# Spreading a finite check over six feed-forward steps of an attention and mixture-of-experts kernel

## The chip, the cores and the metric

The kernel runs on one core of a Trainium2 chip. The time is device microseconds of one execution. Runs of the kernel before took 786.82, 789.31 and 791.52 us, so the median is 789.31 us. The engines are named as in the profile: PE is TensorE (its weight loads are listed as PEld), DVE is VectorE, ACT is ScalarE, POOL is GpSimd and SP is SyncE. Each has its own queue of instructions and takes them in order.

## The reference

Three parts follow one another. Attention keeps, in each row of scores, the 32 largest; a soft mixture of experts with 32 slots follows; last comes a feed-forward layer:

```python
kth = np.partition(scores, -top_k, axis=-1)[..., -top_k:-top_k + 1]
scores = np.where(scores >= kth, scores, -1000000000.0)   # softmax, times v
...
c /= c.sum(1, keepdims=True) + 1e-09                      # mixture: (2304 x 32)
x = c @ slot_out                                          # (2304 x 512)
h = x @ w_in                                              # (512 x 2048)
g = np.where(h >= 1, h, np.where(h <= -1, 0.0, (h + 1) ** 2 / 4.0))
out = g @ w_out                                           # (2048 x 512)
```

Sizes: 4 batches of 8 heads, 576 rows, head width 64; 2304 tokens; 8 experts with a hidden width of 1024; feed-forward width 2048. All in 32-bit floats; the two feed-forward weights come in as 64-bit patterns that the kernel narrows itself.

## The kernel before, in words

Attention runs pair of heads by pair of heads, in an order of operations that is written out by hand (ORDER), and takes the first 480 us or so. Experts and mixture follow to about 545 us. The feed-forward stage is the rest, and the change lies in it.

The feed-forward stage doesn't form x. Since x is c times slot_out, it multiplies slot_out by w_in once and gets a small matrix m (held as four tiles m4[0] to m4[3] of 128 partitions by 512 columns, the "converted weight" of the change), and then h is m times c. m4[0] is made ahead of the stage, m4[1] to m4[3] in steps 4, 12 and 20 (m_spread).

Tokens are cut into six blocks of 384 (t from 0 to 5), the feed-forward width into 16 blocks of 128 (f). A step is one pair (t, f); there are 96. The first 32 steps alternate the blocks t = 0 and 1, and behind them each t goes through its 16 f alone, so steps 32 to 47 are t = 2 and steps 48 to 63 are t = 3. The function step(i) issues, in this order:

- for the pair three steps on (GA = 3), emit_h: one matmul into the PSUM tile h_ps (L1096), on ScalarE the half relu and the square (L1098, L1099);
- for the same pair on VectorE, emit_m (L1104, the last reader of h_ps), the rounded copy of the result (L1112) and the difference from it (L1116), tile names rg and ghl;
- for the pair of step i itself, emit_o: nine matmuls (three for each 128 tokens, L1132) that add into o_ps.

At the last f of a block the three o_ps tiles are copied by ScalarE into o_sb (L1144) and stored by SP (L1145); three buffers serve these copies. While i is below 30, the steps also convert the remaining blocks of w_out (prep, tiles tr_l and whl), with work on ScalarE, VectorE and GpSimd.

PSUM tiles of the tag m_ps have two buffers. h_ps, the tiles of m_spread and the transposes of the checks take them in turn.

The kernel checks two things at run time. tell() looks at whether the shortcut that finds the 32 largest held (bad, badm; L990 and L992), ahead of the feed-forward stage. tell_m() looks at whether m is finite: each of the four tiles is multiplied by zero and summed along its columns (L1000), each sum is compared with zero (L1002), the least of the four is taken in each partition (good, L1004), TensorE turns that column into a row (good_ps, L1006), and VectorE takes its least, turns it about, joins it with badm and writes the one integer flag (L1008 to L1011). At the end every engine reads the flag (L1266), and if it is set, a slow version of the whole kernel runs; with these inputs it doesn't.

The order on TensorE, ScalarE, VectorE and GpSimd is that of the program (manual_schedule). SP's order is set by the scheduler from its model of time; weight loads keep their program order.

Of the kernel before, what the change touches and what calls it, by code (L numbers as in the profile page):

```python
# [8 lines left out]
F32 = mybir.dt.float32  # L9
# [5 lines left out]
ALU = mybir.AluOpType  # L15
AX = mybir.AxisListType
# [3 lines left out]
P = 128  # L20
# [28 lines left out]
NC1 = DFF // CW  # L49
# [30 lines left out]
def kernel_body(tc, qT, kT, vP, phi, w1, w2, w_in, w_out, out, fast, flag):  # L80
    nc = tc.nc
# [3 lines left out]
    ident = cpool.tile([P, P], F32, name="ident")  # L85
# [745 lines left out]
    ps = ps_m.tile([P, P], F32, name="si_ps", tag="m_ps")  # L831
# [17 lines left out]
    m4 = [p_m.tile([P, 512], F32R, name=f"m4_{n}") for n in range(4)]  # L849
    wB = [tail.enter_context(tc.tile_pool(name=f"wB{n}", bufs=1)) for n in range(NB)]  # L850
    p_t = tail.enter_context(tc.tile_pool(name="p_t", bufs=1))
# [37 lines left out]
    mx = {}  # L889
# [102 lines left out]
            nc.vector.reduce_max(badm, ps[:1, :], axis=AX.X)  # L992
            mx["badm"] = badm

    def tell_m():
        if fast:
            sums = p_t.tile([P, NC1], F32, name="sums")
            t = p_t.tile([P, 512], F32, name="none", tag="so_sb", bufs=1)
            for n in range(NC1):
                nc.vector.tensor_scalar(t, m4[n].bitcast(F32), 0.0, 0.0, op0=ALU.mult, op1=ALU.add,  # L1000
                                        accum_out=sums[:, n:n + 1])
            nc.vector.tensor_scalar(sums, sums, 0.0, None, op0=ALU.is_equal)  # L1002
            good = p_t.tile([P, 1], F32, name="good")
            nc.vector.tensor_reduce(good, sums, axis=AX.X, op=ALU.min)  # L1004
            ps = ps_m.tile([P, P], F32, name="good_ps", tag="m_ps")
            nc.tensor.transpose(ps[:1, :], good, ident)  # L1006
            goodm = p_t.tile([1, 1], F32, name="goodm")
            nc.vector.tensor_reduce(goodm, ps[:1, :], axis=AX.X, op=ALU.min)  # L1008
            nc.vector.tensor_scalar(goodm, goodm, -1.0, 1.0, op0=ALU.mult, op1=ALU.add)
            nc.vector.tensor_tensor(goodm, goodm, mx["badm"], op=ALU.max)  # L1010
            nc.vector.tensor_copy(flag, goodm)  # L1011
# [15 lines left out]
    def m_rest():  # L1027
        mx["m"] = ps_m.tile([P, 512], F32, name="m_ps1", tag="m_ps")
        for c in range(NHP):
            for n in range(1, NC1):  # L1030
                nc.tensor.matmul(mx["m"][32 * n:32 * n + 32], so128[:, c, 0, :], wtile[(2, 0, 2 * n + c // 2)][c % 2],
                                 start=(c == 0), stop=(c == NHP - 1), tile_position=(0, 32 * n), skip_group_check=True)

    def m_split():
        mhl = slot_view(h1T_slots[0], "mhl", F32R, [P, 2, 512])
        mh, ml = mhl[:, 0], mhl[:, 1]
        both = (slice(32, 64), slice(64, P))
        for rows in both:
            nc.scalar.copy(mh[rows], mx["m"][rows])
        for rows in both:  # L1040
            nc.vector.tensor_tensor(ml[rows], mx["m"][rows], mh[rows].bitcast(F32), op=ALU.subtract)
        return mh, ml

    def m_spread(n, mh, ml):
        rows = slice(32 * n, 32 * n + 32)
        ps = ps_m.tile([P, 512], F32, name="m_ps2", tag="m_ps")
        for k, part in enumerate((mh, ml)):
            sel = twice[rows, 2 - 2 * k:6 - 2 * k].rearrange("p k s -> p (k s)")
            nc.tensor.matmul(ps, sel, part[rows], start=(k == 0), stop=(k == 1), tile_position=(32 * n, 0))
        nc.scalar.copy(m4[n], ps)  # L1050
# [19 lines left out]
    def prep(f, k):  # L1070
        x64 = wtile[(4, 0, f)]
        hf = x64[:, :, 1].bitcast(F32)
        if k == 0:
            preps[f] = slot_tiles(tr_slots[f % 3], "tr_l", I32)[0]
        t, r = preps[f][:, 0], preps[f][:, 1]
        tf = t.bitcast(F32)
        if k == 0:
            nc.scalar.activation(tf, hf, AF.Abs)
            nc.scalar.activation(r.bitcast(F32), x64[:, :, 0].bitcast(U32), AF.Identity, bias=two, scale=2.0 ** -51)
        elif k == 1:  # L1080
            nc.vector.tensor_scalar(tf, tf, 2.0 ** -15, None, op0=ALU.max)
            nc.vector.tensor_scalar(t, t, 3, None, op0=ALU.logical_shift_left)
            nc.gpsimd.tensor_tensor(t, t, r, op=ALU.add)  # L1083
        elif k == 2:
            nc.vector.scalar_tensor_tensor(t, x64[:, :, 1], SIGN, t, op0=ALU.bitwise_and, op1=ALU.bitwise_or)
            wo_t[f] = slot_tiles(w_slots[f], "whl", F32R)[1]
        elif k == 3:
            nc.scalar.copy(wo_t[f][0], tf)
        else:
            nc.vector.tensor_tensor(wo_t[f][1], tf, wo_t[f][0].bitcast(F32), op=ALU.subtract)  # L1090
            del preps[f]

    def emit_h(s_):
        t, f = s_
        ph = ps_m.tile([P, 512], F32, name="h_ps", tag="m_ps")[:, :BLK]
        nc.tensor.matmul(ph, m4[f // 4][:, f % 4 * P:(f % 4 + 1) * P], cT[t // 3][:, t % 3 * BLK:(t % 3 + 1) * BLK], start=True, stop=True)  # L1096
        r, g = (x[:, :BLK] for x in ring_tile("g", g_slots, "rg", F32))
        nc.scalar.activation(r, ph, AF.Relu, bias=half, scale=0.5)  # L1098
        nc.scalar.activation(r, r, AF.Square)  # L1099
        gs[s_] = ph, r, g  # L1100

    def emit_m(s_):
        ph, r, g = gs[s_]
        nc.vector.scalar_tensor_tensor(g, ph, 1.0, r, op0=ALU.max, op1=ALU.min)  # L1104
        gs[s_] = g, [x[:, :BLK] for x in ring_tile("g", g_slots, "ghl", F32R)]

    def emit_c(s_, on):
        g, (gh, gl) = gs[s_]
        if on is nc.scalar:
            nc.scalar.copy(gh, g)  # L1110
        else:
            nc.vector.tensor_copy(gh, g)  # L1112

    def emit_d(s_):
        g, (gh, gl) = gs[s_]
        nc.vector.tensor_tensor(gl, g, gh.bitcast(F32), op=ALU.subtract)  # L1116
        gs[s_] = gh, gl
# [6 lines left out]
    def emit_o(t, f, rows):  # L1124
        if f == 0:
            pos[t] = [ps_f.tile([P, DM], F32, name=f"o_ps{t}_{n}", tag=("o_ps", "e_ps")[t % 2]) for n in range(NS)]
        gh, gl = gs[t, f]
        wh, wl = wo_t[f]
        for n in rows:
            sl = slice(n * P, (n + 1) * P)  # L1130
            for k, (a, w) in enumerate(((gh, wh), (gh, wl), (gl, wh))):
                nc.tensor.matmul(pos[t][n], a[:, sl], w, start=(f == 0 and k == 0),  # L1132
                                 stop=(f == NF - 1 and k == 2))
            if f == NF - 1:
                o = ring_tile("o", o_slots, "o_sb", F32)[0]
                dst = out[t * BLK + n * P:t * BLK + (n + 1) * P, :]
                if (t, n) == (NT // BLK - 1, NS - 1):
                    a, z = slice(0, DM // 2), slice(DM // 2, DM)
                    nc.scalar.copy(o[:, a], pos[t][n][:, a])
                    nc.vector.tensor_copy(o[:, z], pos[t][n][:, z])  # L1140
                    nc.scalar.dma_start(dst[:, a], o[:, a])
                    nc.sync.dma_start(dst[:, z], o[:, z])
                else:
                    nc.scalar.copy(o, pos[t][n])  # L1144
                    nc.sync.dma_start(dst, o)  # L1145
# [7 lines left out]
    def step(i):  # L1153
        t, f = steps[i]
        nxt = steps[i + GA] if i + GA < len(steps) else None

        def work(*ks):
            for k in ks:
                for x in todo.get((i, k), ()):
                    prep(x, k)  # L1160

        if i == 2:
            m_rest()
            mhl.extend(m_split())
        if i == 40:
            tell_m()
        if i % 8 == 4 and i // 8 < NC1 - 1:
            m_spread(i // 8 + 1, *mhl)
        if i in (0, 2):
            emit_o(t, f, range(NS))  # L1170
        if nxt:
            emit_h(nxt)
        work(4, 2, 1)
        late_g = behind.pop() if behind else None
        if late_g:
            emit_c(late_g, nc.scalar)
        work(3, 0)
        if nxt:
            emit_m(nxt)
        if late_g:  # L1180
            emit_d(late_g)
        if nxt:
            if any((j, 0) in todo for j in (i, i - 1)):
                behind.append(nxt)
            else:
                emit_c(nxt, nc.vector)
                emit_d(nxt)
        if i not in (0, 2):
            emit_o(t, f, range(NS))
# [60 lines left out]
    for i in range(len(steps) - NLAST):  # L1250
        step(i)
# [72 lines left out]
```

## Time and profile before

| | |
|---|---|
| median of three runs | 789.31 us |
| profiled execution, its time | 789.28 us |
| profiled execution, span from first to last instruction | 787.5 us |
| mean granted TensorE clock (share of full speed) | 0.978 |
| TensorE matmul busy | 748.9 us, 95% of the span |
| TensorE weight loads busy | 548.6 us, 70% |
| VectorE busy | 638.4 us, 81% |
| ScalarE busy | 619.7 us, 79% |
| GpSimd busy | 467.2 us, 59% |

The busy shares are averages over stages with different limits. In the page's chain of work that ended last, the o_ps matmuls of L1132 are the largest entry, with 23% of the span; from 548 us on the chain is nearly all theirs. The clock is given as a share of 2.4 GHz: 1.00 is the upper of its two levels, and about 0.50 the lower, 1.2 GHz; a stretch with both lies between.

### The profile page before, as it was taken

The page shows a single profiled execution, that of the slowest core. Times are in us where ns is not written, and L with a number is a line of the kernel's source. Part 1 is how long each engine was busy: PE and PEld are TensorE (multiplying, and loading weights), DVE is VectorE, ACT ScalarE, POOL GpSimd, SP SyncE. Part 2 cuts the span into 40 slices and gives each one's busy share as a digit, 9 for nine tenths or more (in the row PEclk, how much of TensorE's full clock was granted, in tenths as well). Part 3 has the DMA queues.
Part 4 walks back from the last instruction along what each step waited for, and adds up shares of the span by engine and source line. Part 5 has one row for each costly group of instructions (what it writes and reads, how often), then busy time and mean ns, then how long its engine had stood idle before and what let it go on. Part 6 is the DMA issues. An engine that isn't in the chain of part 4 may idle for free.

```text
span 787.5 us, 15936 instructions
## 1 busy us (share of the span) xinstructions
PE 748.9 (95%) x5023; PEld 548.6 (70%) x5023; DVE 638.4 (81%) x2918; ACT 619.7 (79%) x1312; POOL 467.2 (59%) x516
## 2 busy tenths in 40 slices
PE   4899999999999999999999998897999998999996
PEld 2477677777777777777777777333677876888885
DVE  5999999999999999999999973163588866666663
ACT  4799999999999999999999985162699953555552
POOL 2899999999999999999999990020122100000000
PEclk8899999999999999999999999899999998999999
DMA  7414304303312320220220346999500010101101
GB/s 225 146 52 147 130 18 147 135 24 142 134 60 102 134 93 20 80 94 15 96 82 15 90 145 189 347 403 408 215 0 2 29 52 2 41 0 41 37 4 44
DMA packets 31725, 81.50 MB, mean 103 GB/s; under 512 B 5648, under 2 KB 6544, under 8 KB 31632
## 3 DMA queue, kind: packets, MB, share of 16 engines
q1 hardware_dynamic: 31344, 79.94, 28.7%
q8 instruction: 41, 0.67, 0.4%
q14 instruction: 52, 0.43, 0.2%
q10 hardware_dynamic: 288, 0.46, 0.2%
HBM read 71.25 MB, written 8.91 MB: 102 GB/s over the span
## 4 chain that ended last, share of the span: by engine, by line
PE 58%; DVE 19%; ACT 7%; POOL 6%; DMA 5%; issue 2%; SPq 1%; ACTq 0%; DVEq 0%; POOLq 0%
PE o_ps L1132 23%; PE av_ps L502 8%; PE s_ps L294 5%; PE pt_ps L461 5%; DVE cand L318 5%; DMA w<-in_moe_w_dram 4%; DVE top L424 4%; PE x_ps L294 3%; POOL ssb L450 3%; DVE cand L323 2%; PE h_ps L1096 2%; DVE top L325 2%; POOL mb L377 2%; DVE mb L374 2%; PE av_ps L500 1%
## 5 line engine op out<-in xcount | busy, mean ns | idle before, releaser
L1132 PE MATMUL o_ps<-whl,ghl 128*128 128x512 f32 x864 | 219.3, 399 | 0.0
L1132 PEld LDWEIGHTS o_ps<-whl,ghl 128*128 128x128 f32 x864 | 163.4, 191 | 36.0 <-issue 0.8
L450 POOL TENSOR_TENSOR ssb<-ssb,pen 128x576 f32<-128x576 f32 x141 | 180.2, 1283 | 2.5
L318 DVE MAX8 cand<-ssb 128x8 f32<-128x82 f32 (+1 forms) x1008 | 163.7, 235 | 5.7 <-ACT ssb L309 5.7
L502 PE MATMUL av_ps<-v_sb,ptb 128*128 128x65 f32 (+1 forms) x1280 | 143.4, 262 | 0.0
L502 PEld LDWEIGHTS av_ps<-v_sb,ptb 128*128 128x128 f32 (+1 forms) x1280 | 137.7, 182 | 5.8 <-issue 5.8
L1098 ACT ACTIVATE rg<-h_ps,half 128x384 f32<-128x384 f32 x96 | 55.6, 579 | 78.2 <-PE h_ps L1096 78.1
L377 POOL TENSOR_SCALAR mb<-ssb,top 128x576 bf16<-128x576 f32 x64 | 110.2, 1721 | 0.9 <-DVE top L325 0.9
L294 PE MATMUL s_ps<-kt,qt 64*128 64x288 f32 x512 | 100.0, 468 | 8.8 <-ACT ssb L309 4.4
L309 ACT COPY ssb<-s_ps 128x576 f32<-128x576 f32 x144 | 95.7, 665 | 11.3 <-PE s_ps L294 9.9
L461 PE MATMUL pt_ps<-ident,ssb 128*128 128x128 f32 x640 | 100.3, 279 | 2.5 <-ACT ptb L477 2.4
L1083 POOL TENSOR_TENSOR tr_l<-tr_l 128x512 int32<-128x512 int32 x16 | 21.1, 1318 | 127.5 <-PE so L968 42.4
L1104 DVE SCALAR_TENSOR_TENSOR rg<-h_ps,rg 128x384 f32<-128x384 f32 x96 | 53.3, 555 | 53.1 <-ACT rg L1099 53.1
L461 PEld LDWEIGHTS pt_ps<-ident,ssb 128*128 128x128 f32 x640 | 72.0, 146 | 30.3 <-ACT rs L485 6.8
L477 ACT COPY ptb<-pt_ps 128x512 f32<-128x512 f32 x128 | 77.9, 608 | 3.8 <-PE pt_ps L461 3.7
L453 ACT ACTIVATE ssb<-ssb,kn 128x576 f32<-128x576 f32 x96 | 78.4, 816 | 0.7 <-POOL ssb L450 0.6
L447 ACT ACTIVATE pen<-ssb,kn 128x576 bf16<-128x576 f32 x96 | 75.3, 809 | 1.7 <-POOL kn L443 0.9
L424 DVE MAX8 top<-x_ps 128x8 f32<-128x584 f32 x96 | 72.7, 757 | 2.2 <-PE x_ps L408 1.9
L325 DVE MAX8 top<-cand 128x8 f32<-128x56 f32 x432 | 72.8, 205 | 0.1
L294 PEld LDWEIGHTS s_ps<-kt,qt 64*128 64x128 f32 x512 | 39.9, 190 | 34.5 <-ACT ssb L309 10.9
L414 POOL TENSOR_TENSOR w<-ssb,mb 128x576 f32<-128x576 f32 x48 | 61.5, 1281 | 0.4 <-DVE mb L374 0.4
L1116 DVE TENSOR_TENSOR ghl<-rg,ghl 128x384 fp32r<-128x384 f32 x96 | 55.3, 576 | 6.0
(231 smaller groups left out, 1282.5 us busy)
## 6 DMA issues: line engine op xcount, KB each, us to landing
w<-in_moe_w_dram SPq DMA_DIRECT2D x52, 512.0 KB, 6.8
x<-in_moe_w_in_dram SPq DMA_DIRECT2D x16, 512.0 KB, 3.8
w<-in_moe_w_out_dram SPq DMA_DIRECT2D x16, 512.0 KB, 10.2
w<-in_moe_w_dram SPq DMA_DIRECT2D x24, 256.0 KB, 5.4
kt<-in_k_dram SPq DMA_DIRECT2D x15, 360.0 KB, 4.3
v_sb<-in_v_dram SPq DMA_DIRECT2D x16, 325.0 KB, 6.9
qt<-in_q_dram SPq DMA_DIRECT2D x15, 320.0 KB, 5.0
out_dram<-o_sb SPq DMA_DIRECT2D x17, 256.0 KB, 2.2
```

The source lines that it names most:

```text
L294: nc.tensor.matmul(o, q[us], k[us, c:c + o.shape[-1]], start=True, stop=True, tile_position=(j * D, 0), skip_group_check=True)
L309: nc.scalar.copy(ssb[:, 0] if u[1] == NR else ssb[:, :, hf], st.pop((u, hf))[:, :, :HS])
L318: nc.vector.max(st[u]["cand"][:, j, 8 * g:8 * g + 8], row(u, j)[:, S * g // NSEG:S * (g + 1) // NSEG])
L325: nc.vector.max(t8, cand)
L377: nc.gpsimd.tensor_scalar(kept(u, j), row(u, j), t_u, None, op0=ALU.is_ge)
L424: nc.vector.max(st[u]["top"][:, j, TOPU:], src)
L450: nc.gpsimd.tensor_tensor(row(u, j), row(u, j), st.pop((u, "pen", j)), op=ALU.subtract)
L453: nc.scalar.activation(row(u, j), row(u, j), AF.Exp, bias=st[u]["kn"][:, j, 0:1], scale=0.125)
L461: nc.tensor.transpose(pt[:, c, :], pr[:, c0:c0 + P], ident)
L477: nc.scalar.copy(st[u, "ptb", j], st.pop((u, "pt", j)))
L502: nc.tensor.matmul(o, pj[:, c, sl], v_sb[:, 4 * jj + c, :], start=False, stop=(c == NR - 1), skip_group_check=True)
L1132: nc.tensor.matmul(pos[t][n], a[:, sl], w, start=(f == 0 and k == 0), stop=(f == NF - 1 and k == 2))
```

## The change

tell_m is given a number k and does one piece for each: k from 0 to 3 sums one tile of m4, k = 4 compares the sums and takes the least, k = 5 does the transpose and all that follows it. The tiles that pass from piece to piece (sums, good) are kept in the dictionary mx. step(i) calls it at i = 40, 44, 48, 52, 56 and 60, each time ahead of the rest of the step, where the kernel before called the whole at i = 40. The last sum is at step 52, the comparison at 56, the transpose at 60.

```diff
-    def tell_m():
-        if fast:
-            sums = p_t.tile([P, NC1], F32, name="sums")
+    def tell_m(k):
+        if not fast:
+            return
+        if k < NC1:
+            if k == 0:
+                mx["sums"] = p_t.tile([P, NC1], F32, name="sums")
             t = p_t.tile([P, 512], F32, name="none", tag="so_sb", bufs=1)
-            for n in range(NC1):
-                nc.vector.tensor_scalar(t, m4[n].bitcast(F32), 0.0, 0.0, op0=ALU.mult, op1=ALU.add,
-                                        accum_out=sums[:, n:n + 1])
-            nc.vector.tensor_scalar(sums, sums, 0.0, None, op0=ALU.is_equal)
-            good = p_t.tile([P, 1], F32, name="good")
-            nc.vector.tensor_reduce(good, sums, axis=AX.X, op=ALU.min)
+            nc.vector.tensor_scalar(t, m4[k].bitcast(F32), 0.0, 0.0, op0=ALU.mult, op1=ALU.add,
+                                    accum_out=mx["sums"][:, k:k + 1])
+        elif k == NC1:
+            nc.vector.tensor_scalar(mx["sums"], mx["sums"], 0.0, None, op0=ALU.is_equal)
+            good = mx["good"] = p_t.tile([P, 1], F32, name="good")
+            nc.vector.tensor_reduce(good, mx["sums"], axis=AX.X, op=ALU.min)
+        elif k == NC1 + 1:
             ps = ps_m.tile([P, P], F32, name="good_ps", tag="m_ps")
-            nc.tensor.transpose(ps[:1, :], good, ident)
+            nc.tensor.transpose(ps[:1, :], mx["good"], ident)
             goodm = p_t.tile([1, 1], F32, name="goodm")
             nc.vector.tensor_reduce(goodm, ps[:1, :], axis=AX.X, op=ALU.min)
...
-        if i == 40:
-            tell_m()
+        if i % 4 == 0 and i >= 40:
+            tell_m(i // 4 - 10)
```

## Rows read from the trace of the kernel before

**Rows 1.** Chain of waits, 640 to 662 us: start, duration (us), engine, tile, line, count.

```profile
644.23 2.10 PE o_ps L1132 x9
...
649.40 0.61 DVE none L1000 x2
...
652.43 0.17 DVE good L1004
...
652.64 0.37 PE good_ps L1006
...
653.34 3.84 PE o_ps L1132 x9
```

**Rows 2.** Busy time by stretch: stretch, length, engines' busy time (count), clock, DMA.

```profile
644.23:646.50 2.27, 2.27 (x12) 1.86 (x11) 1.48 (x4) 1.11 (x2) 0.00 (x0) 1.00 0.00 0
646.50:653.34 6.84, 2.80 (x13) 2.05 (x12) 5.32 (x15) 1.11 (x2) 0.00 (x0) 0.80 0.00 0
653.34:657.50 4.16, 4.16 (x11) 3.28 (x11) 1.91 (x6) 1.10 (x2) 0.00 (x0) 0.51 0.01 2
657.50:659.77 2.27, 2.27 (x11) 1.87 (x11) 0.92 (x2) 1.10 (x2) 0.00 (x0) 1.00 0.04 11
...
662.06:707.39 45.33, 45.33 (x201) 37.28 (x201) 29.53 (x61) 23.57 (x43) 0.00 (x0) 1.00 0.05 18
```

**Rows 3.** Timeline around step 40: start, duration, engine, line, instruction, idle before it.

```profile
646.17 0.34 PE L1096 MATMUL h_ps<-cT,m 128*128 128x384 f32 x1
...
646.35 2.26 PE L1132 MATMUL o_ps<-whl,ghl 128*128 128x512 f32 x9
...
647.72 0.56 DVE L1104 SCALAR_TENSOR_TENSOR rg<-h_ps,rg 128x384 f32<-128x384 f32 x1 [0.66 <-ACT rg L1099]
...
648.84 0.56 DVE L1116 TENSOR_TENSOR ghl<-rg,ghl 128x384 fp32r<-128x384 f32 x1
649.32 0.68 DVE L1000 TENSOR_SCALAR_CACHE_REDUCE none<-m 128x512 f32<-128x512 f32 x1
...
650.04 0.69 DVE L1000 TENSOR_SCALAR_CACHE_REDUCE none<-m 128x512 f32<-128x512 f32 x1
...
652.23 0.17 DVE L1002 TENSOR_SCALAR sums<-sums 128x4 f32<-128x4 f32 x1
...
652.64 0.37 PE L1006 MATMUL good_ps<-ident,good 128*1 128x128 f32 x1 [4.04 <-DVE good L1004]
...
653.05 0.28 DVE L1008 TENSOR_REDUCE goodm<-good_ps 1x1 f32<-1x128 f32 x1 [0.47 <-PE good_ps L1006]
...
653.72 0.14 DVE L1011 CAST flag<-goodm 1x1 int32<-1x1 f32 x1
```

**Rows 4.** Timeline of TensorE around the transpose of the other check.

```profile
514.92 0.27 PE L990 MATMUL bad_ps<-ident,bad 128*1 128x128 f32 x1
515.12 3.64 PE L968 MATMUL so<-w,h1T 128*32 128x512 f32 x32
```

**Rows 5.** Busy time by stretch: an earlier idle, the steps behind it, forty steady microseconds.

```profile
548.43:552.39 3.96, 3.96 (x12) 3.19 (x12) 3.26 (x7) 1.10 (x2) 0.00 (x0) 0.60 1.03 409
545.65:548.07 2.42, 0.00 (x1) 0.03 (x1) 1.23 (x3) 1.06 (x3) 0.00 (x0) 1.00 1.03 413
...
560.00:600.00 40.00, 38.94 (x169) 30.78 (x168) 32.19 (x64) 37.50 (x73) 9.06 (x7) 1.00 0.04 17
```

**Rows 6.** Timeline of TensorE behind an m_spread: h_ps and its wait.

```profile
564.73 0.44 PE L1096 MATMUL h_ps<-cT,m 128*128 128x384 f32 x1 [0.57 <-DVE rg L1104]
```

**Rows 7.** Instruction groups by line, VectorE, 608 to 646 and 646.5 to 657.5 us.

```profile
L1082 DVE TENSOR_SCALAR tr_l<-tr_l 128x512 int32<-128x512 int32 x3 | 1.3, 427 | 0.1
...
L1000 DVE TENSOR_SCALAR_CACHE_REDUCE none<-m 128x512 f32<-128x512 f32 x4 | 2.7, 684 | 0.1
```

**Rows 8.** Waits of SP's queue (total, times, longest) and the page's output stores.

```profile
SPq L1266 <- DVE flag L1011: 21.8, 1, 21.8
...
out_dram<-o_sb SPq DMA_DIRECT2D x17, 256.0 KB, 2.2
```

## The prediction, made before the changed kernel ran

> **What bounds the kernel now.** I read the chain of waits first, since it says which engine ends last. From 644 us on it is one pattern [rows 1]: a feed-forward step is nine o_ps matmuls of L1132 (2.10 us in the chain) behind one h_ps matmul, and TensorE goes from one group to the next. Once, at step 40, the chain leaves TensorE: it runs through VectorE's ghl L1116, the sums of L1000 and the minimum of L1004, and comes back by the transpose good_ps of L1006. The next group takes 3.84 us in place of 2.10.
>
> Second, the busy time by stretch [rows 2]. Twenty undisturbed steps last 45.33 us, so a step is 45.33 / 20 = 2.267 us; TensorE is busy in all of it at a granted clock of 1.00, while VectorE has 1.48 us of work in a step of 2.27. The two disturbed stretches last 6.84 and 4.16 us. In the second the granted clock is 0.51, the lower of the two levels (1.2 GHz), and directly behind it 1.00 again.
>
> Third, the timeline of step 40, which says who waits for what [rows 3]. TensorE sat idle for 4.04 us ahead of good_ps. Its last work before was the group that starts at 646.35 and takes 2.26, so it came to the transpose at 648.6. VectorE began the first sum only at 649.32, because the three operations of step 39's rg and ghl stand ahead in its queue, and its chain up to good ended at 652.6. So the step waits for VectorE's place in line (0.7 us) and for the chain of six small results (3.3 us). Everything of TensorE's program behind the transpose waits with it. VectorE and ScalarE have nothing to do that would end later.
>
> **What the disturbance costs now.** The stretch from 646.50 to 657.50 holds two steps: 6.84 + 4.16 - 2 x 2.267 = 6.47 us above two normal ones [rows 2]. Of that 4.04 is idle [rows 3]; the rest, 2.43, is the transpose itself and work at the lower clock: 4.16 - 2.27 = 1.89 in the second step, 0.5 around the transpose and the h_ps behind it.
>
> **Part by part.** No instruction is added or removed. The four sums, the comparison with the minimum, and the transpose with its four small operations move from step 40 to the starts of steps 40, 44, 48, 52, 56 and 60. No DMA is issued by them; the flag that two queues read comes later (below).
>
> The sums, steps 40 to 52. Each enters VectorE's queue ahead of that step's rg L1104. It costs 650.04 - 649.32 = 0.72 us from start to start [rows 3]. VectorE waits 0.66 us for ScalarE before each L1104 [rows 3], and this idle time is the cover. Without the check the next L1104 would have started 2.267 after 647.72, at 649.99; behind one sum VectorE is free at 650.04, so L1104 is 0.05 late. The buffers ahead decide whether TensorE sees it. A step makes the operands of the step three later: they were ready at 648.84 + 0.56 = 649.40, and their matmuls would start at 646.35 + 3 x 2.267 = 653.15 in an undisturbed run, 3.75 us later. The two h_ps buffers leave a margin as well: L1104 ends at 647.72 + 0.56 = 648.28, and that buffer is next needed by the h_ps two steps on, 646.17 + 4.53 = 650.70, 2.4 us later. Cost 0. The bounds: below, nothing, since the sums leave VectorE's total work as it is; above, 4 x 0.72 = 2.9 us, if each sum went straight to TensorE. I take 0, because the margin is five times a sum, and three normal steps without a sum follow each, in which the lag is worked off.
>
> At this place stands a row that another price would contradict: tensor_scalar over 128x512 took 427 ns for L1082 and 684 for the summing L1000 [rows 7]. The Trainium skill (VectorE: DVE Perf Modes, The perf-mode tier table) lets tensor_scalar on fp32 in SBUF run at twice the base rate; L1082 looks like that, L1000 does not. By the rule a sum would fit into the idle time with no lag, and the third rival below would have no price; by the row it just fails to fit. I go by the row.
>
> Comparison and minimum, step 56: from 652.23 to the end of L1004, some 0.37 us of VectorE, inside the 0.66 us of idle. Cost 0; if the cover went, 0.37.
>
> The transpose, step 60. It waits for good, which VectorE finished four steps, 9 us, earlier; so TensorE does not stop. Behind it in the queue stand h_ps and nine o_ps matmuls of the step. Its price in a running stream is that of bad_ps, the same instruction for another check: 514.92 to 515.12, 0.20 us [rows 4]. It also takes one turn of the two-buffer PSUM ring. The h_ps behind it now needs the buffer of the step before, not of two steps before. L1104 frees that 2.11 us after its h_ps (646.17 to 648.28), and the next h_ps comes 2.267 + 0.20 = 2.47 after it: margin 0.36 us, no wait. In the earlier steps where such an extra PSUM tile went in while VectorE was also converting weights, the h_ps behind it waited 0.57 us [rows 6]. So the transpose costs 0.20 at least and 0.20 + 0.57 = 0.77 at most; I take 0.20, since VectorE has no conversion left by then. The four small operations (653.05 to 653.86, 0.81 us) stand ahead of one L1104 on VectorE. The transpose ends before VectorE is through with the step before, so they do not wait, and they make that L1104 0.15 late, inside the 3.75.
>
> The flag. SP waited 21.8 us for it, between the sixth and the seventh output store, and read it at 653.9 [rows 8]. Step 40 would begin at 646.17 + 2.267 = 648.44, so the flag comes at about 648.44 + 20 x 2.267 + 1.8 = 695.6. If SP's read keeps its place, the three stores of the third token block wait until then; they land some 2.2 us after their issue [rows 8], by about 699.5. Their buffers are wanted again when the first rows of step 63 are done, about 648.44 + 23 x 2.267 + 0.20 + 1.0 = 701.8. Cost 0, with 2 us to spare. TensorE, VectorE and ScalarE read the flag only after their last work.
>
> **Sum.** -6.47 + 0 + 0 + 0.20 = -6.27 us. The profiled execution took 789.28 us (span 787.5), which is the median of the runs, 789.31, to 0.03. So 789.28 - 6.27 = **783.0 us**, 0.8% faster.
>
> **Rivals.**
> Only the idle goes. If the lower clock after the stall had another cause, 1.89 us would remain: 784.9. For it: the clock record lies beside the stall and does not prove cause. Against: the other long idle of this stage, 2.42 us, was also followed by a slow stretch, at 0.60, while forty steady microseconds ran at 1.00 [rows 5]. Chance 0.05.
>
> The pieces hold TensorE where they now stand. Each costs what it takes on VectorE: 4 x 0.72 + 0.37, and 0.57 more at the transpose, 3.8 us in all: 786.8. For it: at those steps VectorE has 1.48 + 0.72 = 2.20 of 2.27 us to do. Against: the margins of 3.75 and 2.4 us. Chance 0.07.
>
> Slower. The four sums make TensorE pause through the PSUM ring, and every pause lowers the clock for a step: 0.72 + 1.89 = 2.6 us four times, 10.4, so 793.4. It decides from three such pauses on (7.8 against 6.27). The place is the h_ps of each sum step. Against: h_ps waits of 0.57 us in the weight-conversion steps [rows 6] lie in forty microseconds that show 1.00 throughout [rows 5]; a pause would have to be several times longer. The Trainium skill (TensorE: Matmul & The Clock Gate, A second HAM failure mode: psum-queue depth-cycling) describes just this, short idles from cycling PSUM buffers that make the clock swing; by that rule the earlier ring waits should show it, and the trace does not agree. Chance 0.03.
>
> The change gives nothing that shows, because the time is taken elsewhere: SP's later flag read holds stores and through them the copies that empty PSUM. It needs the landing 2 us later than worked out, and then has the 3.75 us margin before it. Time 789, chance 0.02.
>
> **How the numbers follow.** Forecast 0.83; rivals 0.05, 0.07, 0.03, 0.02. A measurement of this kernel tells a change from none at about 0.5%, 3.9 us; the runs of before span 786.8 to 791.5. The forecast's 6.3 us lies outside that, but with this scatter I give it 0.06 of its 0.83 to be read as within 0.5%. Faster: 0.77 + half of the first rival = 0.80. Slower 0.03. Same 0.17. Range: 783.0 less 2.4 for the scatter is 780.6; above, the first rival (784.9) with 1.7 of the scatter gives 786.6 and takes in the transpose's upper bound (783.6).
>
> **What would show it.** In the trace of the changed kernel: no TensorE idle above some tenths between 640 us and the last group; granted clock 1.00 throughout; step 40 to step 59 each 2.27 us; step 60 2.47. L1104 late by 0.05 to 0.2 us at steps 40, 44, 48, 52 and 60 and on time one step later. The flag read at about 695. I am wrong if h_ps waits for L1104 behind the transpose, if the clock falls again, or if the end of the span moves by less than 4 us with the stall gone.

## The result, and the profile after

The changed kernel took 782.39 us (median of six runs, 781.57 to 783.26); the kernel before, 788.82 beside it (786.82 to 791.52). The ratio is 0.9916, 95% interval 0.9896 to 0.9937: 6.4 us less, against 6.3 forecast. The profiled execution took 783.15 us, with a span of 781.3.

The chain of waits of the kernel after, around step 60 (start, duration, engine, tile, line, count), answers to [rows 1]:

```profile
691.56 2.09 PE o_ps L1136 x9
693.65 0.11 PE good_ps L1010
693.76 0.18 PE h_ps L1100
693.94 2.10 PE o_ps L1136 x9
```

From 584 us to the last o_ps group the chain no longer leaves TensorE, and the transpose is 0.11 us of it. The busy time by stretch (stretch, length, busy time of the engines, clock, DMA) answers to [rows 2]; the rows are twenty steps from step 40 on, without the transpose; from the o_ps group of step 59 to that of step 60, with the transpose; the step behind it; and the rest up to the last groups:

```profile
648.52:693.82 45.30, 45.30 (x202) 37.19 (x202) 32.12 (x70) 23.57 (x43) 0.00 (x0) 1.00 0.05 18
691.40:693.77 2.37, 2.37 (x12) 1.86 (x12) 1.50 (x4) 1.11 (x2) 0.00 (x0) 1.00 0.00 0
693.77:696.04 2.27, 2.27 (x11) 1.86 (x11) 2.03 (x8) 1.10 (x2) 0.00 (x0) 1.00 0.00 0
696.20:766.39 70.19, 70.19 (x312) 57.82 (x311) 45.71 (x93) 37.19 (x68) 0.00 (x0) 1.00 0.06 23
```

The twenty steps that now hold the sums take 45.30 us, as twenty undisturbed ones did (45.33), at clock 1.00. From the start of one o_ps group to the next, step 60 takes 2.37 in place of 2.27. The timeline of steps 40 and 60 answers to [rows 3]:

```profile
648.59 0.56 DVE L1120 TENSOR_TENSOR ghl<-rg,ghl 128x384 fp32r<-128x384 f32 x1
649.07 0.68 DVE L1002 TENSOR_SCALAR_CACHE_REDUCE none<-m 128x512 f32<-128x512 f32 x1
...
649.73 0.56 DVE L1108 SCALAR_TENSOR_TENSOR rg<-h_ps,rg 128x384 f32<-128x384 f32 x1
...
651.98 0.56 DVE L1108 SCALAR_TENSOR_TENSOR rg<-h_ps,rg 128x384 f32<-128x384 f32 x1 [0.64 <-ACT rg L1103]
...
693.49 0.27 PE L1010 MATMUL good_ps<-ident,good 128*1 128x128 f32 x1
693.49 0.19 PEld L1100 LDWEIGHTS h_ps<-cT,m 128*128 128x128 f32 x1 [0.15 <-DVE rg L1108]
...
694.37 0.27 DVE L1012 TENSOR_REDUCE goodm<-good_ps 1x1 f32<-1x128 f32 x1
...
695.14 0.56 DVE L1108 SCALAR_TENSOR_TENSOR rg<-h_ps,rg 128x384 f32<-128x384 f32 x1
```

The sum at 649.07 fills VectorE's idle time: the L1108 behind it shows no wait, and the next has its 0.64 us of idle again. At step 60 no TensorE matmul waits. The weight load of h_ps shows 0.15 us of idle, which the profile puts down to L1108. That L1108 had ended some 0.16 us before (it started at 692.77 and took 0.56), and the load started together with the transpose at 693.49; so the row doesn't show a wait for the PSUM ring. In SP's waits (total, times, longest) the flag comes later, as in [rows 8]:

```profile
SPq L1270 <- DVE flag L1015: 27.8, 1, 27.8
```

It was read at 695.2, so SP waited from 667.4 on.

### The profile page after: what moved, and what is told of

Read it like the earlier page. It is cut to its first block, busy times and chain, and to the rows that moved or that the text cites. A ratio compares the mean times of both kernels' runs of the same rounds, so it can differ in the third digit from the quotient of the medians.

```text
span 781.3 us, 15935 instructions
## 1 busy us (share of the span) xinstructions
PE 746.4 (96%) x5023; PEld 547.2 (70%) x5023; DVE 638.0 (82%) x2918; ACT 619.8 (79%) x1312; POOL 467.2 (60%) x516
## 4 chain that ended last, share of the span: by engine, by line
PE 64%; DVE 17%; ACT 7%; POOL 7%; DMA 3%; issue 2%; ACTq 0%; POOLq 0%; DVEq 0%; SPq 0%
PE o_ps L1136 25%; PE av_ps L502 9%; PE s_ps L294 6%; PE pt_ps L461 5%; DVE cand L318 5%; DVE top L424 4%; PE x_ps L294 3%; POOL ssb L450 3%; PE h_ps L1100 2%; PE h L945 2%; POOL mb L377 2%; DVE cand L323 2%; DVE top L325 2%; DVE mb L374 2%; PE av_ps L500 1%
## 5 line engine op out<-in xcount | busy, mean ns | idle before, releaser
L1108 DVE SCALAR_TENSOR_TENSOR rg<-h_ps,rg 128x384 f32<-128x384 f32 x96 | 53.4, 556 | 47.9 <-ACT rg L1103 47.8
```

## The experiments

Medians are set against runs of the kernel before on the same chip and in the same rounds; 1 us is 0.13%. Executions of one kernel scatter by some 2 us, so each kernel is also read by one stretch of its trace: from the start of the second o_ps group of the feed-forward stage to the start of the last 27 o_ps matmuls, as the chain of waits gives it. It leaves out what varies earlier, with one exception: in the double sums the second o_ps group itself still ran partly at the lower clock (2.82 us in place of 2.25), so that stretch holds some 0.6 us from there. The kernel before took 788.82 us beside the kernel after, 789.23 beside the first four experiments and 789.33 beside the next four.

| kernel | median us | ratio to before, 95% | stretch us |
|---|---|---|---|
| before | 789.23 | | 773.07 - 552.39 = 220.68 |
| after | 782.39 | 0.9896 to 0.9937 | 766.39 - 552.13 = 214.26 |
| no check | 782.49 | 0.9909 to 0.9948 | 764.43 - 550.25 = 214.18 |
| sums together at step 40 | 782.62 | 0.9909 to 0.9936 | 765.64 - 551.06 = 214.58 |
| transpose at once, step 56 | 783.75 | 0.9922 to 0.9952 | 767.08 - 551.46 = 215.62 |
| before, wait filled | 787.13 | 0.9969 to 0.9992 | 769.67 - 551.10 = 218.57 |
| nine transposes | 785.24 (one run) | | 768.72 - 553.64 = 215.08 |
| longer wait, step 56 | 787.03 | 0.9956 to 0.9987 | 769.15 - 550.55 = 218.60 |
| double sums at step 40 | 787.53 | 0.9969 to 1.0000 | 770.57 - 551.29 = 219.28 |

**No check.** In the kernel after, the pieces are taken out:

```diff
-        if i % 4 == 0 and i >= 40:
-            tell_m(i // 4 - 10)
+        if i == 60 and fast:
+            nc.vector.tensor_copy(flag, mx["badm"])
```

> The kernel after with the whole finite check of m left out: the flag is written from badm alone, at step 60. Theory (the spread pieces cost TensorE nothing but one transpose of 0.1 to 0.2 us): 782.2 to 782.3 us, not to be told from the kernel after (782.4); step 60 takes 2.27 us in place of 2.38. Rival (each piece holds TensorE for what it takes on VectorE, 3.8 us in all): 778.6.

Measured 782.49 us; the stretch is 214.26 - 214.18 = 0.08 us shorter, and the theory expected 0.1 to 0.2. So the check costs TensorE some 0.1 us where it now stands, and another place for it could win no more than that. The rival's 778.6 falls.

**Sums together, transpose late.** The spread is undone and only the transpose's new place kept:

```diff
-        if i % 4 == 0 and i >= 40:
-            tell_m(i // 4 - 10)
+        if i == 40:
+            for k in range(NC1 + 1):
+                tell_m(k)
+        if i == 60:
+            tell_m(NC1 + 1)
```

> The kernel after with the four sums, the comparison and the minimum together at step 40, and only the transpose left at step 60. Theory (the wait of TensorE was for the transpose; the margins ahead carry a late VectorE): the chain of 3.3 us makes L1108 of step 40 2.6 us late; the h_ps two steps on needs its buffer 2.4 us after it was normally free, so TensorE waits 0.2 to 0.5 us at step 42 and the clock stays 1.00: 782.6 to 782.9. Rival (the spreading is what brought the gain, and a chain of 3.3 us on VectorE stalls TensorE wherever the transpose stands): near 788.8, with a stretch at the lower clock.

Measured 782.62 us; the stretch is 0.32 us longer than after. The timeline of steps 40 to 42, and the busy time from the o_ps group of step 41 to that of step 42:

```profile
651.15 0.16 DVE L1007 TENSOR_REDUCE good<-sums 128x1 f32<-128x4 f32 x1
651.23 0.55 DVE L1108 SCALAR_TENSOR_TENSOR rg<-h_ps,rg 128x384 f32<-128x384 f32 x1
651.83 0.19 PEld L1100 LDWEIGHTS h_ps<-cT,m 128*128 128x128 f32 x1 [0.45 <-DVE rg L1108]
```

```profile
649.57:652.11 2.54, 2.53 (x12) 1.78 (x11) 2.33 (x8) 1.11 (x2) 0.00 (x0) 1.00 0.00 0
```

The h_ps two steps on did wait for its buffer, and cost 2.54 - 2.27 = 0.27 us at clock 1.00. So moving the transpose alone brings 220.68 - 214.58 = 6.10 us of the 6.42, and with it moved, spreading the sums adds the other 0.32.

**Transpose at once.** Everything as after, but the transpose follows the minimum in step 56:

```diff
-        if i % 4 == 0 and i >= 40:
+        if i % 4 == 0 and 40 <= i < 60:
             tell_m(i // 4 - 10)
+        if i == 56:
+            tell_m(NC1 + 1)
```

> The kernel after with the transpose at step 56, directly behind the comparison and the minimum of the same step. Theory (TensorE waits at the transpose until VectorE has come through its queue): VectorE is free 0.9 us into the step and needs 0.37, so TensorE sits idle about 1.3 us. If the clock stays at 1.00 the time is 783.7; if it falls as it did behind an idle of 2.4 us, 785.6 to 786.1. The theory says the idle; which of the two the clock does is open, since waits of 0.57 us left it at 1.00. Rival (the sums alone were the cost and the place of the transpose is free): 782.4, no idle.

Measured 783.75 us, as the theory said for a clock that stays; the stretch is 1.36 us longer than after. The timeline's transpose, and the stretch behind it:

```profile
685.07 0.27 PE L1010 MATMUL good_ps<-ident,good 128*1 128x128 f32 x1 [1.13 <-DVE good L1007]
```

```profile
685.35:687.62 2.27, 2.27 (x11) 1.87 (x11) 1.57 (x6) 1.11 (x2) 0.00 (x0) 1.00 0.00 0
```

The chain is 0.37 us, yet TensorE idles 1.13: the rest is VectorE's own work of the step before, ahead in its queue. In this execution an idle of 1.13 us left the clock at 1.00.

This kernel is also the other half of the change by itself: the sums are spread, and the transpose still follows at once. It brings 220.68 - 215.62 = 5.06 us. So either half alone wins most of the 6.42, and the gains overlap: moving the transpose is worth 6.10 us with the sums together and 1.36 with the sums spread; spreading the sums is worth 5.06 or 0.32.

**The wait, filled.** In the kernel before, matmuls without a use run in the wait:

```diff
-            ps = ps_m.tile([P, P], F32, name="good_ps", tag="m_ps")
-            nc.tensor.transpose(ps[:1, :], good, ident)
+            ps = ps_m.tile([P, 512], F32, name="good_ps", tag="m_ps")
+            for _ in range(16):
+                nc.tensor.matmul(ps, m4[0][:, :P], m4[0], start=True, stop=True)
+            nc.tensor.transpose(ps[:1, :P], good, ident)
             goodm = p_t.tile([1, 1], F32, name="goodm")
-            nc.vector.tensor_reduce(goodm, ps[:1, :], axis=AX.X, op=ALU.min)
+            nc.vector.tensor_reduce(goodm, ps[:1, :P], axis=AX.X, op=ALU.min)
```

> The kernel before with 16 extra matmuls of 128x512 (into the PSUM tile that the transpose then overwrites) ahead of the transpose at step 40, so that TensorE works through the wait; at 0.23 us each they fill 3.7 of the 4.04 us. Nothing is left out. Theory (the lower clock came from the idle): no stretch below 1.00 behind step 40; the wait itself stays; 788.8 less 2.3 to 2.4 is 786.4 to 786.5. Rival (the lower clock has another cause than the idle, so only the idle counts): the slow step of 4.16 us stays, 788.8.

Measured 787.13 us, ratio 0.998: less than before, by 0.6 to 2.4 us. The stretch is 220.68 - 218.57 = 2.11 us shorter. The transpose's row, and the stretches with the wait and behind it:

```profile
651.41 0.27 PE L1008 MATMUL good_ps<-ident,good 128*1 128x128 f32 x1 [0.38 <-DVE good L1004]
```

```profile
645.11:651.69 6.58, 6.20 (x28) 4.78 (x28) 5.10 (x15) 1.11 (x2) 0.00 (x0) 1.00 0.00 0
651.69:653.97 2.28, 2.28 (x12) 1.87 (x11) 1.58 (x6) 1.11 (x2) 0.00 (x0) 1.00 0.03 7
```

With TensorE at work the transpose still starts 651.41 - 645.11 = 6.30 us behind the start of the group before it (6.29 in the kernel before [rows 3]), but the step behind it takes 2.28 us at clock 1.00, where it took 4.16 at 0.51 [rows 2]. The lower clock came from the idle.

**Nine transposes.** In the kernel after:

```diff
-            nc.tensor.transpose(ps[:1, :], mx["good"], ident)
+            for _ in range(9):
+                nc.tensor.transpose(ps[:1, :], mx["good"], ident)
```

> The kernel after with the transpose of step 60 issued nine times, into the same tile. One was forecast at 0.20 us from another check's row; the chain of the kernel after shows 0.11. If a transpose costs 0.11 in this stream, step 60 grows by 0.9 us to 3.3; if 0.20, by 1.6 to 4.0; if the one was partly hidden or a wait for the PSUM ring was in it, by less than 0.5.

One run took 785.24 us (its feed-forward stage began later; its stretch is 0.82 us longer than after). The timeline of TensorE:

```profile
694.94 1.15 PE L1011 MATMUL good_ps<-ident,good 128*1 128x128 f32 x9
...
695.84 0.42 PE L1101 MATMUL h_ps<-cT,m 128*128 128x384 f32 x1
```

Eight more cost 0.82 / 8 = 0.10 us each, so 0.10 to 0.11 is the price in this stream and 0.20 was too much.

**A longer wait.** The kernel with the transpose at step 56, with two sums more ahead of the comparison:

```diff
         elif k == NC1:
+            for n in range(2):
+                t = p_t.tile([P, 512], F32, name="none", tag="so_sb", bufs=1)
+                nc.vector.tensor_scalar(t, m4[n].bitcast(F32), 0.0, 0.0, op0=ALU.mult, op1=ALU.add,
+                                        accum_out=mx["sums"][:, n:n + 1])
```

> The kernel with the transpose at step 56 directly behind comparison and minimum, and two further sums (of tiles 0 and 1 again) ahead of these, so that TensorE's idle ahead of the transpose grows from 1.13 by 2 x 0.72 to 2.6 us. Theory (idle and the fall of the clock behind it are separate prices, and an idle of 1.1 us is too short for the fall while 2.4 us mostly, not always, brings it): 785.2 us where the clock stays, 786.6 to 787.1 where it falls; the median nearer the upper. Rival (only idles as long as 4 us lower it, the start of the stage has another cause): 785.2.

Measured 787.03 us (785.09 to 790.40), at the upper value. The transpose's row, and the two stretches behind it:

```profile
685.61 0.27 PE L1014 MATMUL good_ps<-ident,good 128*1 128x128 f32 x1 [2.59 <-DVE good L1011]
```

```profile
685.90:689.30 3.40, 3.40 (x11) 2.72 (x11) 2.18 (x7) 1.11 (x2) 0.00 (x0) 0.63 0.01 2
689.30:691.97 2.67, 2.67 (x11) 2.17 (x11) 1.05 (x3) 1.10 (x2) 0.00 (x0) 0.83 0.01 3
```

An idle of 2.59 us was followed by steps of 3.40 and 2.67 us: 1.5 us above normal. The rival, that only idles near 4 us lower the clock, falls.

**Double sums.** The kernel with the sums together, each sum done twice (the tile of sums is made once):

```diff
-            if k == 0:
+            if "sums" not in mx:
                 mx["sums"] = p_t.tile([P, NC1], F32, name="sums")
...
-            for k in range(NC1 + 1):
+            for k in (0, 1, 2, 3, 0, 1, 2, 3, NC1):
                 tell_m(k)
```

> The kernel with all sums at step 40 done twice, eight in all, then comparison and minimum; the transpose stays at step 60. VectorE's chain is 8 x 0.72 + 0.37 = 6.1 us, and L1108 of step 40 is 5.5 us late. Theory (the h_ps ring is what ends last, with a margin of 2.2 to 2.4 us): TensorE waits 3.1 to 3.3 us at the h_ps of step 42, and by its length the clock falls behind it: 787 to 788 (785.6 if the clock stayed). Rival (the operands made three steps ahead end last, margin 3.75): a wait of 1.75 us at the o_ps of step 43, 784.2 to 785.6.

Measured 787.53 us. The row of the h_ps that waited, and the stretch behind it:

```profile
655.49 0.69 PE L1100 MATMUL h_ps<-cT,m 128*128 128x384 f32 x1 [2.92 <-DVE rg L1108]
```

```profile
655.98:659.31 3.33, 3.33 (x11) 2.68 (x11) 2.98 (x7) 1.10 (x2) 0.00 (x0) 0.65 0.02 5
```

TensorE waits for a buffer of the h_ps ring, 2.92 us, not 1.75 for operands. The ring, with its margin of 2.4 us, is what a late VectorE meets first.

**Another idle, filled.** A version that could beat both: in the kernel after, TensorE idles 2.4 us ahead of the third h_ps of the feed-forward stage. Matmuls without a use fill it; they write the o_ps tiles of t = 0, which are therefore made earlier.

```diff
-        if f == 0:
+        if f == 0 and t not in pos:
...
+    pos[0] = [ps_f.tile([P, DM], F32, name=f"o_ps0_{n}", tag="o_ps") for n in range(NS)]
+    for k in range(10):
+        nc.tensor.matmul(pos[0][k % NS], m4[0][:, :P], cT[0][:, :DM], start=True, stop=True)
     emit_h(steps[2])
```

> The kernel after with ten extra matmuls of 128x512 ahead of the third h_ps of the feed-forward stage, where TensorE sits idle for 2.4 us in every trace (they write o_ps tiles that the first real group then overwrites). Nothing is left out. At 0.23 us each they fill 2.3 us. In the kernel after the step behind this idle ran at a low clock: 4.10 us from its first o_ps group to the second, against 2.80 in the run without the check, where the clock stayed at 1.00 behind the same idle. Theory (the low clock follows from TensorE's idle, in most runs but not all): clock 1.00 there, 1.3 us less in most runs: 781.0 to 781.4 in the median, and less scatter between runs. Rival (idle and low clock only coincide): no change, 782.4.

Measured 781.81 us (781.55 to 784.51), ratio 0.9895 to 0.9927: not told apart from after. So both were run in the same rounds:

> The kernel after, unchanged, on the same chip and in the same rounds as the next kernel, so that the two can be compared directly. Theory: 782.4 us; runs with the clock down behind the idle of 2.4 us at the start of the stage lie 1.3 us above the others.

> The kernel with the ten extra matmuls in the idle at the start of the feed-forward stage, again. Theory: the clock stays at 1.00 there, and the median is 1.0 to 1.3 us below that of the kernel after in the same rounds. Rival (the median of the kernel after already has most runs with the clock up, or the fill costs what it saves): within 0.5 us of it.

Measured 783.38 us (782.06 to 784.80) for the kernel after and 783.34 (782.34 to 784.73) with the fill. No gain; the theory's 1.0 to 1.3 us didn't come, and the rival's "within 0.5 us" holds. In this second profile of the kernel after the clock stayed up behind the same idle (stretch 214.30 us), so there was nothing to win in that execution. In the ten profiles of this document without the fill, the idle there was 2.42 or 2.43 us each time; the stretch behind it took 3.67 to 4.11 us at a clock of 0.58 to 0.70 in seven, and 2.79 or 2.80 us at 1.00 in three. In both profiles with the fill it took 2.79 or 2.80 at 1.00. So the fill may well save a part of a microsecond on average; six runs of each, which scatter by 2.4 to 2.7 us, don't show it and don't exclude it.

## Why the prediction was right

**The bound and its price.** The forecast was that TensorE waits for the transpose's operand and that the two disturbed steps cost 6.47 us. In the stretch, 220.68 - 214.26 = 6.42 us went with the stall, and 220.68 - 214.18 = 6.50 where the check is left out whole. The two parts were separated: filling the wait gave back 2.11 us, the clock's share (forecast 2.43, which also held the transpose and the h_ps behind it); the rest is the wait. That the median, 782.39, came within 0.6 us of the forecast time is in part luck, since runs of one kernel scatter by more than that; the stretch, 6.42 us against 6.27, is the better test.

**The sums.** Forecast at nothing, with VectorE late by 0.05 us at a sum step. At step 40 it was 0.02 us late (649.73, where 651.98 less one step of 2.267 is 649.71). Twenty steps with them take 45.30 us. The margins that made it so were measured from the other side: a chain of 3.3 us costs 0.3, one of 6.1 us makes TensorE wait 2.92. In the sentence on margins 3.75 and 2.4 us stood side by side; the smaller, of the h_ps ring, is the one that binds. The prediction's "five times a sum" is the larger; the smaller is 2.4 / 0.72 = 3.3 times. The L1082 beside which it set the price of a sum works on integers; on 32-bit floats, L1081 of the kernel before took 418 ns, so the comparison stands.

**The transpose.** Forecast 0.20, measured 0.10 to 0.11: the row of bad_ps [rows 4] stands among matmuls of another shape; that this is why it took 0.20 there wasn't tested. The wait for the PSUM ring was forecast at none, and no matmul of step 60 shows one. Step 60 was forecast at 2.47 and took 2.37.

**The flag.** Forecast at about 695.6, read at 695.2. "If SP's read keeps its place" didn't hold: SP waited only from 667.4, behind the stores of the third token block. It cost nothing either way.

**The rivals.** That only the idle goes is refuted by the filled wait; that the pieces hold TensorE, by the kernel without the check. The slower one, in which ring waits swing the clock, needs a wait far beyond what the pieces cause: the 0.45 us of the sums together left 1.00, 2.92 us did not. The Trainium skill (TensorE: Matmul & The Clock Gate, A second HAM failure mode: psum-queue depth-cycling) speaks of frequent short idles between groups of matmuls; the short ring waits of this kernel don't bear that out, and the one of 2.92 us is single and long.

## What to carry to other kernels

A small result that crosses from one engine to another can cost the consumer what stands ahead of it in the producer's queue, not the chain alone (1.13 us of idle for 0.37 us of work). Issued four steps after its operand was made, the transpose was nearly free here, at 0.1 us. Where TensorE is the bound, price an idle of a few us with the steps behind it: 4.04 us here cost some 6.5. Of two changes made together, test each alone: moving the consumer by itself brought 6.10 us and spreading the producer by itself 5.06, of 6.42 for both, so the gain can't be shared out between them.

## What the runs showed of the hardware

The same idle did not always lower the clock. The rows are the h_ps behind the idle at the start of the stage and the stretch behind it, in the kernel after, and then in the kernel without the check, whose program is the same up to step 40:

```profile
547.73 0.41 PE L1100 MATMUL h_ps<-cT,m 128*128 128x384 f32 x1 [2.43 <-DVE rg L1108]
```

```profile
548.03:552.13 4.10, 4.10 (x12) 3.37 (x12) 3.31 (x7) 1.10 (x2) 0.00 (x0) 0.58 1.03 410
```

```profile
547.15 0.42 PE L1100 MATMUL h_ps<-cT,m 128*128 128x384 f32 x1 [2.42 <-DVE rg L1108]
```

```profile
547.45:550.25 2.80, 2.80 (x13) 2.00 (x13) 2.70 (x6) 1.21 (x3) 0.00 (x0) 1.00 1.03 408
```

Behind 2.42 or 2.43 us of idle the clock was 0.58 in the one and 1.00 in the other, 1.3 us apart; the second profile of the kernel after, with 2.43 us of idle there, also stayed at 1.00, and over the ten profiles without a fill it fell in seven. The first slices differ in the same way, from the pages of the two kernels (clock in tenths of full speed in 40 slices):

```profile
PEclk8899999999999999999999999899999999999998
```

```profile
PEclk9999999999999999999999999899999999999999
```

The Trainium skill (TensorE: Matmul & The Clock Gate, Part 1: The HAM clock gate) says that the slow phase at the start varies from run to run of one kernel. These traces agree (the first slice at 8 tenths in the one, at 9 in the other), and show the same for the fall. Such steps of 1 to 2 us can make a good part of the scatter of 2 to 4 us between runs: of the first six runs of the kernel after, the three with a mean granted clock of 0.993 or more took 781.57 to 781.95 us, the three with 0.989 or less 782.84 to 783.26. In the second six the order is less clean, and that the clock makes all of the scatter wasn't shown.
